# Two attention layers in one planned program: whole-bank writes in the planner for the score maxima, identity products on TensorE before one projection, and a new table of offsets

## The chip, the core and the metric

The kernel runs on one core of one Trainium2 chip. The metric is device time in microseconds (us) of one execution. Several engines work side by side on their own in-order instruction streams: TensorE (PE in the profile, PEld for its weight loads), VectorE (DVE), ScalarE (ACT), GpSimd (POOL) and SyncE (SP), which issues the transfers. PSUM, in which TensorE leaves its results, is used as eight banks of 128x512 float32.

## The reference

Two layers of 2048 tokens, width 1024 and 32 heads of width 32 are computed on separate inputs; their outputs are put side by side.

```python
# A: softmax attention within each of 4 segments of 512 tokens, mixed by a gate with a memory of
#    the segments before
logits = einsum("bhqd,bhkd->bhqk", qs, ks) * scale + mask
a_dot = einsum("bhqk,bhkd->bhqd", softmax(logits), vs)
pq = phi(qs)                                 # phi(t) = t + 1 where t > 0, else exp(t)
a_mem = einsum("bhld,bhde->bhle", pq, M) / (einsum("bhld,bhd->bhl", pq, z)[..., None] + 1e-6)
o = g * a_mem + (1.0 - g) * a_dot
M = M + einsum("bhld,bhle->bhde", phi(ks), vs);  z = z + einsum("bhld->bhd", phi(ks))
...
# B: linear attention with learned features, over all tokens at once
phi_q, phi_k = [concat(softmax(t @ w_phi), softmax(-t @ w_phi)) for t in (q, k)]
kv = einsum("bhsf,bhsd->bhfd", phi_k, v);  z = einsum("bhsf->bhf", phi_k)
o = einsum("bhqf,bhfd->bhqd", phi_q, kv) / (einsum("bhqf,bhf->bhq", phi_q, z)[..., None] + 1e-6)
# each layer ends with o @ wo
```

## The kernel before

**Precision and sizes.** A float32 operand of a large product is held as two float16 halves, and a product of two such operands is three float16 products that add up in one PSUM bank (`product`, the call to TensorE is line 496). Most large products are 128x128 by 128x512. In layer B and in A's output projection, two-by-two block products are made with seven multiplications in place of eight (`strassen`, line 710, and the last loop, line 1805): three banks X, Y and Z are filled, read out by ScalarE and VectorE (lines 716 and 720), and X and Z are then added to again.

**Stages.** Layer A comes first, in 32 units (a segment by a group of four heads), as two functions. `produce(u)` projects queries, keys and values. `attend(u)` finds for each block of queries the largest masked score (`maxima`: products on line 999, VectorE's masked maximum on line 1005, two to four blocks to a bank), turns the 16 maxima of each query into rows that are appended to the operands (line 1024), makes the scores again with the maximum subtracted (line 1104), the exponentials (ACT lines 1108 and 1110, DVE line 1111), the products with the values (line 1140, summed by DVE on line 1144), the normalisation (line 1160), and a transposition by an identity product (line 1172). Preparation of layer B's weights and inputs (`fold`, `prepare`, `weights_v`) is strewn between the units.

Layer B's keys and values follow in eight token pairs: `strassen`, the two softmaxes (`expo`, lines 1395 to 1408), and products that add up the sums over tokens (line 1556; VectorE adds them to `kva`, `ez` and `za` on line 1565).

Then comes the turn from sums to outputs. Each of 16 blocks of 128 queries, numbered c, needs the finished sums: `za` is spread over partitions by float32 identity products (line 1579) into `zb`; the sums `kva` and `ez` (heads 0 to 15 and 16 to 31) are scaled (line 1597) and halved into `kls` (ACT 1599, DVE 1601); the query features `e` of each half hb of the heads are multiplied with `zb` (1710), summed (1713), divided (1716 to 1722), scaled (1724), halved into `eh`, which lies in slot S13 (ACT 1731, and DVE or POOL 1734), transposed by a transfer into `pt` (1737), and multiplied with `kls` (line 1746, 48 short products into the banks `pv` and `kv`: the numerators). Their halves go to `ot` (ACT 1755, DVE 1757), and `project` multiplies `ot` with the output weights: 48 products of line 496 into `misc` banks. While the first of these chains runs, TensorE has the query products of blocks 0 to 3 to make (`strassen`, called for every second c). The output projection of layer A closes the program.

**What sets the order.** The program isn't written in the order in which it runs. Every instruction is recorded by `op` with its engine, an assumed duration, a priority, and what it reads (`r`) and writes (`w`), and `Graph.run` plans them like a list scheduler: an instruction may be placed when, by the assumed durations and latencies, all that it depends on is ready, and the smallest priority goes first. The recorded reads and writes are the planner's alone. The semaphores that the engines wait for are set by the layer below, from the tiles that the instruction really touches. A read or write may name a part of a buffer, as in `(mt, (h, i))`; parts with different keys don't depend on one another. The priority of a job (a run of recorded instructions of one written priority) is shifted by the table `MOVES`, one column of offsets for each engine:

```python
prio += MOVES.get(eng, {}).get(self.job[1], 0.0)
```

The program opens with 56 float32 products of the identity with itself (line 1328), planned at 0.25 us each, while the first inputs are on their way.

Of the kernel before, what the change touches and what calls it, by code (L numbers as in the profile page):

```python
# [379 lines left out]
SP, PE, ACT, DVE, POOL = "SP", "PE", "ACT", "DVE", "POOL"  # L380
# [3 lines left out]
def tile_kernel(ctx: ExitStack, tc: tile.TileContext, ax, aw, awv, awo, beta, bx, bwqk, bwv, bphi, bwo, out):  # L384
    nc = tc.nc
# [71 lines left out]
    op = G.op  # L457
# [512 lines left out]
    def attend(u):  # L970
# [20 lines left out]
        def maxima(*blocks):  # L991
# [11 lines left out]
            for h, i, o in at:  # L1003
                n = 128 * i + 128
                dve(0.073 + 0.001125 * n, lambda h=h, i=i, o=o, n=n: nc.vector.tensor_tensor_reduce(  # L1005
                    ps()[:, o:o + n], ps()[:, o:o + n], causal[:, 512 - n:512], 1.0, NEG, OP.add, OP.max,
                    mt()[:, h, i:i + 1]), w=[(mt, (h, i)), (ps, i)])
# [869 lines left out]
```

## Time and profile before

| | |
|---|---|
| median of 3 runs | 1676.51 us (1674.89 to 1676.59) |
| profiled execution, its own time | 1675.73 us |
| span from first to last instruction in the profile | 1674.0 us |
| mean granted TensorE clock | 0.997 |
| PE busy | 1633.2 us, 98% of the span |
| DVE busy | 1355.2 us, 81% |
| ACT busy | 1120.9 us, 67% |
| POOL busy | 1062.9 us, 63% |

The profile gives each instruction's line, engine, duration, the time its engine was idle before it, and what ended that idle time. A float32 product stands in the trace as two matmul records, so the 56 products of line 1328 are 112 records. The granted clock is TensorE's alone. Times in a window or a timeline are counted from the start of the span. A line of the changed kernel lies 3 lower in the text up to `project` (999 becomes 1002), 6 lower from there to the numerators (1746 becomes 1752), and 10 lower after them.

### The profile page before, as it was taken

How to read it: one execution, taken by the hardware profiler on the slowest of the kernel's cores; microseconds unless marked ns; L12 is line 12 of the kernel's file. 1: busy time of each engine (PE TensorE's matmuls, PEld its weight loads, DVE VectorE, ACT ScalarE, POOL GpSimd, SP SyncE). 2: the span in 40 equal slices, each digit the busy share in tenths (PEclk: the TensorE clock that was granted, in tenths of full speed). 3: DMA queues.
4: the chain of work that ended last, by engine and by line, in shares of the span. 5: the costliest groups of instructions: out<-in, count | busy, mean ns of one | idle time of the engine just before them, and what ended most of it. 6: DMA issues, size and time to landing. Idle time of an engine off the chain costs nothing.

```text
span 1674.0 us, 40119 instructions
## 1 busy us (share of the span) xinstructions
PE 1633.2 (98%) x14964; PEld 963.1 (58%) x14964; DVE 1355.2 (81%) x3187; ACT 1120.9 (67%) x2096; POOL 1062.9 (63%) x1453
## 2 busy tenths in 40 slices
PE   8999999999999999999999999999979999999999
PEld 6666756766676676667665444445534444444444
DVE  6999899998998877798874898778999888964451
ACT  7789979795978878678744676766445555543341
POOL 4667878866689988778541767636478897730000
PEclk9999999999999999999999999999989999999999
DMA  6866765787866576755457364467546768872321
GB/s 211 224 175 151 250 185 169 226 212 191 229 166 210 154 197 210 200 172 157 104 159 274 123 223 164 154 219 283 195 101 166 182 171 183 212 181 99 108 88 69
DMA packets 291410, 299.18 MB, mean 179 GB/s; under 512 B 169088, under 2 KB 222336, under 8 KB 284560
## 3 DMA queue, kind: packets, MB, share of 16 engines
q1 hardware_dynamic: 291216, 296.63, 61.1%
q8 instruction: 117, 1.92, 0.5%
q14 instruction: 77, 0.63, 0.1%
HBM read 161.17 MB, written 86.05 MB: 148 GB/s over the span
## 4 chain that ended last, share of the span: by engine, by line
PE 43%; DVE 5%; ACT 1%; DMA 1%; POOL 0%; issue 0%; DVEq 0%; ACTq 0%
PE proj L710 17%; PE misc L496 9%; PE proj L1805 5%; PE s L710 3%; PE s L1805 2%; PE misc L710 2%; PE misc L1805 1%; PE kv L1556 1%; DVE mx L1395 1%; PE pv L1746 1%; DMA pt<-S 1%; DVE S L1734 1%; DVE pt L1549 1%; DMA wf_d<-oT 0%; DVE r L1405 0%; DVE s L1005 0%
## 5 line engine op out<-in xcount | busy, mean ns | idle before, releaser
L496 PE MATMUL proj<-S,S 128*128 128x128 f16 (+1 forms) x3072 | 500.5, 299 | 2.8 <-ACT S L529 1.2
L496 PEld LDWEIGHTS <-S 128*128 128x128 f16 x4608 | 327.7, 97 | 152.7 <-issue 9.8
L710 PE MATMUL proj<-S,S 128*128 128x512 f16 x1584 | 365.2, 380 | 3.9 <-ACT cs L716 2.4
L710 PEld LDWEIGHTS <-S 128*128 128x128 f16 x2016 | 192.5, 98 | 224.1 <-issue 7.8
L1111 DVE SCALAR_TENSOR_TENSOR ph<-s,ph 128x512 f16<-128x512 f32 x320 | 210.4, 682 | 50.6 <-ACT ph L1110 48.3
L1005 DVE CUSTOM_DVE_ANT_0 s<-s,causal 128x512 f32<-128x512 f32 (+3 forms) x512 | 240.9, 513 | 8.8 <-PE s L999 5.0
L1117 POOL TENSOR_SCALAR_AFFINE_SELECT ph<-ph 128x256 f16<-128x256 f16 (+1 forms) x448 | 195.1, 458 | 76.6 <-DVE ph L1111 58.5
L1110 ACT ACTIVATE ph<-s 128x512 f16<-128x512 f32 x320 | 191.9, 657 | 1.3 <-POOL fo L609 0.4
L496 PE MATMUL misc<-S,ot 128*128 128x512 f16 x768 | 172.2, 379 | 0.0
L1402 ACT ACTIVATE e<-e,sk 128x256 f32<-128x256 f32 x256 | 112.4, 496 | 67.0 <-DVE e L1399 64.2
L496 PEld LDWEIGHTS <-ot 128*128 128x128 f16 x768 | 73.5, 98 | 87.2
L1104 PE MATMUL s<-S 104*128 104x512 f16 (+3 forms) x512 | 117.0, 299 | 2.7 <-DVE amem L1049 0.7
L999 PE MATMUL s<-S 96*128 96x512 f16 (+3 forms) x512 | 111.2, 299 | 3.4 <-ACT pk L952 1.0
L1108 ACT ACTIVATE s<-s,os 128x512 f32<-128x512 f32 x160 | 105.7, 705 | 12.8 <-PE s L1104 12.7
L1108 ACT ACTIVATE s<-s,bd 128x512 f32<-128x512 f32 x160 | 108.0, 721 | 2.5 <-PE s L1104 2.4
L496 PE MATMUL proj<-wv,S 128*128 128x128 f16 x1536 | 108.2, 219 | 0.4 <-DVE ph L1111 0.4
L1140 PEld LDWEIGHTS <-ph 128*128 128x128 f16 x2560 | 87.8, 96 | 20.5 <-issue 2.8
L1140 PE MATMUL pv<-vl,ph 128*128 128x66 f16 (+1 forms) x2560 | 92.3, 184 | 1.5 <-ACT pk L952 0.7
L1405 DVE TENSOR_REDUCE r<-e 128x32 f32<-128x1024 f32 x64 | 76.7, 1207 | 18.0 <-ACT e L1402 17.9
L1710 POOL TENSOR_TENSOR e<-e,zb 128x512 f32<-128x512 f32 x62 | 82.5, 1350 | 12.4 <-ACT zb L1582 7.2
L1005 DVE DVE_READ_ACCUMULATOR2_ANT mt<- 128x1 f32 x512 | 72.4, 141 | 0.0
L1514 POOL TENSOR_TENSOR e<-e,r 128x1024 f32<-128x1024 f32 x32 | 62.1, 1943 | 14.4 <-DVE r L1408 10.0
(345 smaller groups left out, 3259.9 us busy)
## 6 DMA issues: line engine op xcount, KB each, us to landing
S<-xf_d SPq DMA_DIRECT2D x126, 256.0 KB
S<-h SPq DMA_DIRECT2D x192, 128.0 KB
S<-wf_d SPq DMA_DIRECT2D x21, 1024.0 KB
st<-bwqk SPq DMA_DIRECT2D x64, 256.0 KB
out<-os SPq DMA_DIRECT2D x40, 256.0 KB
S<-aw SPq DMA_DIRECT2D x16, 512.0 KB
wa_d<-S SPq DMA_DIRECT2D x16, 512.0 KB
wf_d<-fo SPq DMA_DIRECT2D x32, 256.0 KB
```

Of the source, the lines that this page charges most:

```text
L496: op(PE, dur, lambda c=c, a=a, b=b, lv=lv, rv=rv: nc.tensor.matmul(pv(), lv(), rv(), start=(c == 0 and a + b == 0), stop=(c == n - 1 and a ...
L710: op(PE, 0.215, lambda n=n, a=a, b=b, lv=lv, rv=rv: nc.tensor.matmul(ps(), lv(), rv(), start=(start and n == 0 and a + b == 0), stop=(n == ...
L999: nc.tensor.matmul(ps()[:, o:o + 128 * i + 128], st()[0:96, 0, h, 128 * i:128 * i + 128], st()[0:96, 1, h, 0:128 * i + 128], start=True, s ...
L1005: dve(0.073 + 0.001125 * n, lambda h=h, i=i, o=o, n=n: nc.vector.tensor_tensor_reduce(ps()[:, o:o + n], ps()[:, o:o + n], causal[:, 512 - ...
L1104: nc.tensor.matmul(ps()[:, o:o + n], st()[0:104, 1, h, 128 * j:128 * j + 128], st()[0:104, 0, h, 128 * j:512], start=True, stop=True)
L1108: act(0.59, lambda: nc.scalar.activation(ps(), ps(), AF.Exp, bias=0.0, scale=bdv()[:, 3, i2, 0:1]), r=[(bd, i2)], w=[ps])
L1110: act(0.48, lambda: nc.scalar.activation(ph()[:, 0], ps(), AF.Copy, scale=2.0 ** 14), r=[ps], w=[(ph, 0)])
L1111: dve(0.6, lambda: nc.vector.scalar_tensor_tensor(ph()[:, 1], ps(), 2.0 ** 14, ph()[:, 0], op0=OP.mult, op1=OP.subtract), r=[ps, (ph, 0)], ...
L1117: nc.gpsimd.affine_select(pd, pd, pattern=[[0, n], [1, 128]], compare_op=OP.is_ge, fill=0.0, base=0, channel_multiplier=-1)
L1140: nc.tensor.matmul(ps()[:, i, n0:n1], ph()[:, a, o:o + 128], vl()[:, j, h, n0:n1], start=(i == 0 and a == 0), stop=(j == min(i, 2)), skip_ ...
L1402: op(ACT, 0.41, lambda i=i: nc.scalar.activation(e()[:, 4 * i:4 * i + 4], e()[:, 4 * i:4 * i + 4], AF.Exp, bias=0.0, scale=sk()[:, i:i + 1 ...
L1805: op(PE, 0.215, lambda n=n, a=a, b=b: nc.tensor.matmul(ps(), v(a)[:, n, :], wform[w]()[:, b, n, :], start=(start and n == 0 and a + b == 0 ...
```

## The change

Four edits.

1. In `maxima`, the masked maximum is recorded as a writer of the whole bank and no longer of a part of it. The instruction is the same; in the planner two maxima of one bank now follow one another with the assumed latency of 0.13 us between dependent VectorE instructions.
2. In block c = 0, ahead of each half's numerators, 14 float32 products of the identity with itself are recorded that write the numerators' bank `pv`, which the numerators then overwrite. For the planner they read both lower parts of that half's `eh`.
3. In block c = 0, ahead of the projection's first product, 10 more of the same kind write its `misc` bank. For the planner they read the lower parts of the second half's `eh`.
4. The whole table `MOVES` has other numbers. The set of other instructions stays: the counts by line are equal on every engine but TensorE, which has 38 more.

The products of edits 2 and 3 are planned at 0.11 us each. The matmul itself touches only `ident` and the bank, so that no wait for `eh` is built from it.

```diff
 MOVES = {
     "DVE": {
-        0: -8.8, 4: -25.3, 7: 1.6, 8: -0.7, 10: -2.9, 12: -20.2, 13: 24.6, 14: -1.3, 15: -10.6, 16: -16.6, 17: 0.6, 18: 0.7,
...
+        0: -9.7, 4: -16.8, 7: -26.6, 9: 18.9, 10: 0.1, 12: -0.5, 13: 19.3, 14: 7, 15: -2.1, 16: 6.5, 17: -4.1, 18: 41.3,
...
@@ maxima
                     ps()[:, o:o + n], ps()[:, o:o + n], causal[:, 512 - n:512], 1.0, NEG, OP.add, OP.max,
-                    mt()[:, h, i:i + 1]), w=[(mt, (h, i)), (ps, i)])
+                    mt()[:, h, i:i + 1]), w=[(mt, (h, i)), ps])
@@ project
-    def project(o, w, row, col, prio):
+    def project(o, w, row, col, prio, warm=None):
         for n in range(2):
             ps = bank("misc", [128, 512])
+            for _ in range(0 if warm is None or n else 10):
+                op(PE, 0.11, lambda ps=ps: nc.tensor.matmul(ps()[:, 0:128], ident, ident, start=True, stop=True),
+                   r=warm, w=[ps], prio=prio)
             product((ps, ps), o, at(w[n]), NG, prio, dur=0.215)
@@ the numerators, for each half hb of block c
+            if c == 0:
+                for _ in range(14):
+                    op(PE, 0.11, lambda pn=pn, hb=hb: nc.tensor.matmul(pn[0]()[:, 2 * hb, :], ident, ident, start=True, stop=True),
+                       r=[(eh, (hb, 1, 0)), (eh, (hb, 1, 1))], w=[pn[0]], prio=P)
             op(PE, 0.5, f, r=[(kls, (0, hb)), (kls, (1, hb)), pt], w=pn, prio=P)
@@ the projection of block c
-        project(lambda a, g: (ot, None, lambda otv=otv: otv()[:, a, g, :]), bo, c * 128, 1024, P + 1.1)
+        project(lambda a, g: (ot, None, lambda otv=otv: otv()[:, a, g, :]), bo, c * 128, 1024, P + 1.1, None if c else [(eh, (1, 1, 0)), (eh, (1, 1, 1))])
```

The order moves everywhere. Three places matter here. The first is TensorE's stream just ahead of the first numerators of block 0, in the kernel before; `proj` is a bank of the query products, `pv` and `kv` are the numerators' banks:

```order
L710 MATMUL proj<-S_19191,S_15152 128x512
L710 LDWEIGHTS S_15152
L710 MATMUL proj<-S_19191,S_15152 128x512
L1746 LDWEIGHTS kls
L1746 MATMUL pv<-pt,kls 32x128
```

and in the changed one:

```order
L713 LDWEIGHTS S_15102
L713 MATMUL proj<-S_19242,S_15102 128x512
L1758 MATMUL pv<-ident 128x128 x14
L1621 MATMUL misc<-ident 128x128 x10
L713 LDWEIGHTS S_15102
L713 MATMUL proj<-S_19242,S_15102 128x512
L713 LDWEIGHTS S_15102
L713 MATMUL proj<-S_19242,S_15102 128x512
L713 LDWEIGHTS S_19695
L713 MATMUL proj<-S_19357,S_19695 128x512
L1752 LDWEIGHTS kls
L1752 MATMUL pv<-pt,kls 32x128
```

The ten products that were recorded for the projection stand here too, ahead of the first numerators, since the second half's `eh` was planned to be ready early. Ahead of these rows there are 103 query products after the last key sums, and 104 before. The other 14 stand between the two halves' numerators.

The second place is TensorE's stream right behind the second half's numerators, before:

```order
L1746 LDWEIGHTS kls
L1746 MATMUL kv<-pt,kls 32x128
L710 LDWEIGHTS S_14196
L710 MATMUL proj<-S_19002,S_14196 128x512
```

and now:

```order
L1752 LDWEIGHTS kls
L1752 MATMUL kv<-pt,kls 32x128
L499 LDWEIGHTS ot
L499 MATMUL misc<-S_19831,ot 128x512
```

Before, 12 query products, the numerators of block 1 and 12 more query products stood between block 0's numerators and its projection; now the projection (48 products, `misc` from `ot`) follows at once, and the numerators of block 1 come behind it.

The third place is VectorE's stream from the last but few instructions to the second part of `kls` (`ez` is the second half's sum, `mx`, `e` and `r` are of the query softmax, `S13` is `eh`), before:

```order
L1601 TENSOR_TENSOR kls_19785<-kva_16712,kls_19785 128x512
L1395 TENSOR_REDUCE mx_20009<-proj_19636 128x16 x2
L1399 TENSOR_TENSOR e_20066<-mx_20009,proj_19636 128x16x32
L1734 TENSOR_TENSOR S13_19903<-e_19759,S13_19903 128x512
L1597 TENSOR_TENSOR ez_16875<-ez_16875,zr_19773 128x512
L1405 TENSOR_REDUCE r_20074<-e_19988 128x32
L1734 TENSOR_TENSOR S13_19903<-e_19574,S13_19903 128x512
L1601 TENSOR_TENSOR kls_19785<-ez_16875,kls_19785 128x512
```

and now:

```order
L1604 TENSOR_TENSOR kls_19787<-kva_16748,kls_19787 128x512
L1740 TENSOR_TENSOR S13_19952<-e_19499,S13_19952 128x512 x2
L1600 TENSOR_TENSOR ez_16903<-ez_16903,zr_19755 128x512
L1400 TENSOR_TENSOR e_19989<-s_19897,mx_19943 128x16x32
L1402 TENSOR_TENSOR e_19989<-mx_19943,s_19897 128x16x32
L1398 TENSOR_REDUCE mx_20007<-proj_19675 128x16
L1402 TENSOR_TENSOR e_20019<-mx_20007,proj_19675 128x16x32
L1604 TENSOR_TENSOR kls_19787<-ez_16903,kls_19787 128x512
```

From the last write of `za` to this second part of `kls`, VectorE had 56 instructions before and has 50 now; two of block 1's lower halves (`S13` from `e_19759` and `e_19574` before) have moved behind it, and so have four reductions of line 1395 and one bank addition of line 720. The start of the program (the 56 products and the first products after them) is unchanged on TensorE.

225 rows, old and new, of the table MOVES are left out of this document.

## The prediction

> **What bounds the kernel now.** I read the busy shares first, then TensorE's busy time by stage, then its waits, and last the one stage that stands out, instruction by instruction. The page's first part:
>
> ```profile
> PE 1633.2 (98%) x14964; PEld 963.1 (58%) x14964; DVE 1355.2 (81%) x3187; ACT 1120.9 (67%) x2096; POOL 1062.9 (63%) x1453
> ```
>
> TensorE is the bound: all its idle time together is 1674.0 - 1633.2 = 40.8 us, 2.4% of the span. No reordering can gain much more, and products that are added anywhere but in idle time cost their whole length. By stage (window, PE busy, PEld, DVE, ACT, POOL, granted clock, DMA):
>
> ```profile
> 0.00:850.00 850.00, 826.66 (x8890) 573.42 (x8891) 744.26 (x2146) 686.54 (x1260) 639.93 (x1011) 1.00 0.67 189
> 850.00:1200.00 350.00, 348.65 (x2526) 179.73 (x2525) 275.29 (x500) 219.80 (x446) 193.45 (x205) 1.00 0.60 201
> 1200.00:1250.00 50.00, 38.36 (x348) 17.13 (x347) 47.53 (x81) 22.70 (x47) 36.15 (x38) 0.90 0.49 138
> 1250.00:1650.00 400.00, 399.64 (x3116) 184.08 (x3114) 285.91 (x459) 188.41 (x340) 193.40 (x201) 1.00 0.56 150
> 1650.00:1674.00 24.00, 19.91 (x93) 8.78 (x90) 2.25 (x3) 3.44 (x5) 0.00 (x0) 1.00 0.17 66
> ```
>
> TensorE idles 23.3 us in layer A's first 850 us, 1.4 in the key stage, 11.6 in the 50 us of the turn, 0.4 in the outputs and 4.1 at the end. Only the first and the third can give anything. In the first the idle time is crumbs; the largest groups of the waits (total, times, longest):
>
> ```profile
> PE misc L1024 <- POOL mh L1022: 3.6, 8, 1.2
> PE pv L1746 <- ACT kls L1599: 3.4, 1, 3.4
> PE pv L1746 <- DVE kls L1601: 2.8, 2, 2.2
> PE misc L1328 <- DVE ident L416: 2.6, 1, 2.6
> PE proj L710 <- ACT cs L716: 2.4, 3, 1.4
> PE pv L1746 <- DMA pt<-S: 2.0, 2, 1.8
> PE proj L710 <- DVE s L720: 1.5, 1, 1.5
> ...
> PE s L999 <- DVE ph L1111: 0.9, 1, 0.9
> ```
>
> In the turn it is a few long waits, and a slow clock. TensorE's timeline (start, length, work, idle before it):
>
> ```profile
> 1200.31 9.66 PE L710 MATMUL proj<-S,S 128*128 128x512 f16 x44
> 1211.47 7.93 PE L710 MATMUL proj<-S,S 128*128 128x512 f16 x36 [1.50 <-DVE s L720]
> 1220.83 2.75 PE L710 MATMUL proj<-S,S 128*128 128x512 f16 x12 [1.43 <-ACT cs L716]
> 1224.33 2.75 PE L710 MATMUL proj<-S,S 128*128 128x512 f16 x12 [0.74 <-ACT cs L716]
> 1228.87 0.23 PE L1746 MATMUL pv<-pt,kls 64*32 64x128 f16 x1 [1.79 <-DMA pt<-S]
> ...
> 1229.74 0.23 PE L1746 MATMUL pv<-pt,kls 64*32 64x128 f16 x1 [0.57 <-DVE kls L1601]
> ...
> 1233.56 0.29 PE L1746 MATMUL pv<-pt,kls 64*32 64x128 f16 x1 [3.39 <-ACT kls L1599]
> ...
> 1236.18 0.28 PE L1746 MATMUL pv<-pt,kls 64*32 64x128 f16 x1 [2.21 <-DVE kls L1601]
> ...
> 1236.74 4.67 PE L710 MATMUL proj<-S,S 128*128 128x512 f16 x12
> ```
>
> Beside it VectorE's last write of the key sums and its last part of `kls`, and the issues of the transposing transfers:
>
> ```profile
> 1199.00 0.15 DVE L1565 SCALAR_TENSOR_TENSOR za<-kv,za 128x4 f32<-128x4 f32 x1
> ...
> 1234.49 1.63 DVE L1601 TENSOR_TENSOR kls<-ez,kls 128x512 f16<-128x512 f32 x1
> ```
>
> ```profile
> 1224.40 4.44 SPq L1737 DMA_TRANSPOSE pt<-S  x2
> ```
>
> The seven waits are 1.50 + 1.43 + 0.74 + 1.79 + 0.57 + 3.39 + 2.21 = 11.6 us, the whole idle time of that stage. Behind them 12 products take 4.67 us where 12 took 2.75. The windows say why:
>
> ```profile
> 1227.00:1230.40 3.40, 0.80 (x49) 0.38 (x48) 3.40 (x5) 2.40 (x6) 2.07 (x2) 1.00 1.14 211
> 1230.40:1240.60 10.20, 4.83 (x58) 1.91 (x59) 10.13 (x15) 5.96 (x14) 7.60 (x6) 0.50 0.74 161
> 1240.60:1244.00 3.40, 3.40 (x62) 1.66 (x61) 2.52 (x4) 0.59 (x2) 2.29 (x5) 1.00 0.27 77
> ```
>
> Behind 3.4 us in which TensorE was busy for 0.80, the clock is halved for 10.2 us; 4.83 us of work stood in them and would have taken 2.4. So the turn loses 11.6 + 2.4 = 14.0 us.
>
> **The change part by part.**
>
> *The identity products.* One product costs what the opening's do:
>
> ```profile
> 13.65 4.71 PE L1328 MATMUL misc<-ident 128*128 128x128 f32 x40
> ```
>
> That is 20 products in 4.71 us, their 40 records less than 0.12 apart: 0.23 us each, about twice the 0.11 us that the planner was told. The 24 ahead of the first numerators take 5.5 us, the 14 between the halves 3.2, together 8.7. They wait for no other engine: their reads of `eh` are the planner's, so they run when TensorE arrives. Before, it arrived at 1224.33 + 2.75 = 1227.1. Of the waits ahead of that, 1.43 and 0.74 were for a bank's read-out between two multiplications into one bank; the new order puts 8 other products (8 x 0.22 = 1.8 us, the rate of the 44 in 9.66) into each of those places, so both waits go. The 1.50 stays, as I see nothing that moves it. Arrival is then about 1224.7 (a query product less), the 24 end at 1230.2, three query products follow, and the first numerators start at 1230.9.
>
> Are they ready then? VectorE ran without a pause there (47.53 of 50 us), so I step through its rows. Lower parts of the first half: the steps of the rows from `za` to there sum to 21.8 us before (0.6 for 512 elements, 1.13 for 1024, 0.1 to 0.26 for the short ones) and took about 25.2, since some rows lasted longer while POOL ran (below). Now the steps sum to 22.9, so some 26.3, at 1225.4; the transfers took 1228.87 - 1224.40 = 4.5 us to land, so `pt` is there at 1229.9. Ready. Second part of `kls`: the steps summed to 31.0 and took 37.0 (1236.12 - 1199.15); now they sum to 26.5, so about 32, at 1231.2 to 1232.2. The row of 1.63 us at 1234.49 shows the stretching: its work is 0.6, the rest lies under this POOL row:
>
> ```profile
> 1234.15 1.42 POOL L1734 TENSOR_TENSOR S<-e,S 128x512 f16<-128x512 f32 x1 [2.46 <-ACT S L1731]
> ```
>
> The first numerators take 0.5, the 14 products 3.2, so the second numerators start at 1234.6, ready, and end at 1235.1, against 1236.8 before. Here the 3.39 and 2.21 are gone, and so is the reason for the half clock.
>
> What is late next is the projection, which now follows at once. `ot` needs two ACT and two DVE rows behind the numerators:
>
> ```profile
> 1236.87 0.60 ACT L1755 ACTIVATE ot<-pv 128x512 f16<-128x512 f32 x1 [2.85 <-PE kv L1746]
> ...
> 1238.11 0.68 DVE L1757 SCALAR_TENSOR_TENSOR ot<-kv,ot 128x512 f16<-128x512 f32 x1
> ```
>
> 1238.79 less the 1236.8 at which the numerators ended, and 0.2 to TensorE: 2.2 us of idle time. Before, 12 query products covered it; now nothing does, since the ten products meant for it stand ahead of the first numerators. Behind it 48 products run, long enough for block 1's numerators.
>
> The turn then loses 8.7 (added products) + 1.5 + 2.2 = 12.4 in place of 14.0: **-1.6 us**. Bounds: if VectorE's rows come early enough that neither the 1.5 nor the 2.2 is left, -5.3; if `kls` comes as late as before (1236.1), TensorE idles 1.5 more, and if the clock is halved as well, 10.2 us of dense work lose up to 5.1: +5.0.
>
> *The whole-bank rule and the offsets in layer A.* The rule changes no instruction. In the new order a bank's two maxima mostly have one of another bank between them. VectorE's rows there cost:
>
> ```profile
> L1005 DVE CUSTOM_DVE_ANT_0 s<-s,causal 128x512 f32<-128x512 f32 x128 | 91.8, 717 | 5.0 <-PE s L999 5.0
> ```
>
> Its time is the same in either order; only the bank is held for one row longer. The offsets can take away at most the stage's idle time less the opening's 2.62 and 1.2, some 19.5 us, and can add as much again. I compared, in TensorE's stream, the work that stands between products that hang together through other engines: the least between a unit's rows and its scores is 6.9 us of products now and was 6.2, between scores and their value products 4.3 against 3.0; between the last maxima product and the rows 3.0 against 3.3, where the waits of line 1024 arise. Two of three have more room, none much. VectorE, at 744 of 850 us the second bound, has 13 to 20 us less work ahead of the ends of units 15 and 17, and 7 more ahead of those of units 1 and 18 (the order's instructions, each at its line's busy time over its count). I take a tenth of the crumbs: **-2 us**, with -8 and +8 as ends. Key stage, outputs and end have 1.4, 0.4 and 4.1 us of idle time and the same loops: 0.
>
> *Sum.* -1.6 - 2.0 = -3.6 on the profiled execution's 1675.73, which gives 1672.1; that execution was 0.8 below the median of the runs, so **1673** against the median of 1676.5.
>
> *A rule against this.* The Trainium skill (TensorE: Matmul & The Clock Gate, section "HAM oscillation — how this bites in real kernels") has it that only an idle gap over about 3.4 us brings the half clock. By that the wait of 1.79 us needed no cover: the 24 products ahead of the first numerators are 5.5 us for nothing but the waits that they happen to fill, and the 14 alone would do. The trace disagrees on the threshold: the clock fell at 1230.4, a few tenths into the 3.39 us wait, behind a stretch that was a quarter busy. By the rule the new 2.2 us gap is harmless; by the row it is not certainly so.
>
> **The rivals.**
>
> *The clock falls all the same*, in the projection's wait: 2.2 us idle and half a microsecond of numerators could make a 3.4 us stretch as thin as the 0.80 above. Then up to 5.1 us come back: 1678. Against it: the identity products are dense up to the numerators, so such a stretch is some 35% busy.
>
> *Slower: a bank held too long.* The whole-bank rule makes the short maximum stand behind another bank's longest, 0.72 us later. Where TensorE has no spare `s` bank, its next maxima or scores wait. This can happen 4 times in each of 32 units; it decides from about one in ten: 13 x 0.72 = 9 us, 1682. For it: TensorE already waits on VectorE at line 999 (0.9 us above), and the work between a unit's first and last maxima product grew from 6.7 to 7.7 us in the middle. Against it: the planner holds banks by the same rule, so that it sees the wait.
>
> *The order pays off in layer A.* With VectorE's early load lightened, half of the 19.5 us go: 1666.
>
> *The change does nothing that can be told.* The waits move and the identity products cost what the clock gave: 1676.5.
>
> **How the numbers follow.** Forecast, a small gain at 1673: 0.47 (0.27 faster, 0.20 the same). Clock falls, 1678: 0.13 (0.09 the same, 0.04 slower). Bank held, 1682: 0.17, slower. Layer A pays off, 1666: 0.15, faster. Nothing, 1676.5: 0.08 (0.01, 0.05, 0.02). With 0.2% (3.4 us) as what can be told from no change: faster 0.43, the same 0.34, slower 0.23. The forecast's own range is 1669 to 1677; the unknown ends and the rivals on both sides make it 1664 to 1683.
>
> **What would show it.** Right: identity products of 0.23 us, the clock at 1.00 throughout the turn, no wait of over 2.5 us at the numerators, a wait of about 2 us for `ot` at the projection, and some 21 us of idle time in the first 850. Wrong: a granted clock of 0.5 in the turn; numerators that still wait for `kls`; idle time at lines 999 and 1104 that grows on VectorE's account; or a first half that moves by more than 8 us, which would mean that the table, of which I can judge least, decides.

## The result, and the profile after

| | before | after |
|---|---|---|
| median of the runs beside each other | 1676.55 us (1674.89 to 1678.01, 6 runs) | 1665.64 us (1664.21 to 1666.33, 6 runs) |
| span of the profiled execution | 1674.0 us | 1663.4 us |
| ratio of the times, 95% interval | | 0.9937 [0.9927, 0.9947] |

The change makes the kernel faster by 10.9 us. A small gain to 1673 was forecast: the direction is right, and the gain is three times as large as forecast. The result lies outside the forecast's own range of 1669 to 1677, and inside the whole range of 1664 to 1683 that the rivals made, near its lower end.

The page's first part for the changed kernel:

```profile
PE 1636.6 (98%) x15040; PEld 971.7 (58%) x15040; DVE 1345.6 (81%) x3187; ACT 1119.8 (67%) x2096; POOL 1062.7 (64%) x1453
```

TensorE's idle time fell from 40.8 us to 1663.4 - 1636.6 = 26.8, while its busy time rose by 3.4 with the identity products. The stages, in the windows of the kernel before (columns: window, PE busy, PEld, DVE, ACT, POOL, granted clock, DMA share, GB/s):

```profile
0.00:850.00 850.00, 831.56 (x9036) 580.46 (x9037) 745.78 (x2174) 694.56 (x1274) 642.37 (x1023) 1.00 0.68 191
850.00:1200.00 350.00, 349.84 (x2427) 177.66 (x2426) 268.75 (x493) 217.77 (x442) 194.03 (x197) 1.00 0.60 203
1200.00:1250.00 50.00, 46.51 (x427) 25.82 (x425) 43.33 (x69) 20.19 (x41) 38.91 (x42) 0.97 0.42 107
```

Idle in them: 18.4, 0.2 and 3.5 us, against 23.3, 1.4 and 11.6. Read like that, the turn would seem to have given the most, 8.1 us. It has not: TensorE is busy there with products that are not part of the result. What a stage gave is read from a mark at its end. The last product of the key sums (line 1556) ends 10.2 us earlier than before (1187.2 against 1197.4), and the last product of the program 10.6 us earlier (1659.4 against 1669.9). Nearly all the gain is made **before the turn begins**.

To see where, I took for each TensorE instruction the time from its start to the start of the next, less the median of that step for the same line and shape in the kernel before, and summed it by stage. This counts a stretched step as lost, which a sum of idle time does not. Layer A loses 35.6 us where it lost 44.7 (units 0 to 7: 20.1 against 19.7; 8 to 15: 6.5 against 10.4; 16 to 23: 5.2 against 8.8; 24 to 31: 3.8 against 5.8), the key stage 1.3 against 2.5. So 9.1 us come from layer A and 1.2 from the key stage. In layer A the loss at line 1024 went from 6.9 to 4.8, at 1140 from 4.1 to 2.6, at 1067 from 2.8 to 1.0, at 1042 from 2.9 to 1.4, at 1104 from 6.4 to 5.3, and at 999 from 7.6 up to 9.1. No single place gave more than 2.1 us. In a second execution of the changed kernel (below) layer A loses 37.2 us by the same sum, 7.5 less than before.

The waits of the changed kernel (total, times, longest) hold nothing on `kls` any more, where the longest waits of before were:

```profile
PE misc L1027 <- POOL mh L1025: 2.8, 6, 0.9
PE proj L713 <- DVE s L723: 2.7, 1, 2.7
PE misc L1331 <- DVE ident L419: 2.6, 1, 2.6
PE s L1002 <- ACT pk L955: 1.5, 2, 0.9
...
PE misc L499 <- ACT ot L1765: 0.7, 1, 0.7
```

The turn in TensorE's timeline (start, length, work, idle before it), with the identity products on lines 1758 and 1621:

```profile
1189.44 14.46 PE L713 MATMUL proj<-S,S 128*128 128x512 f16 x65
1206.58 9.70 PE L713 MATMUL proj<-S,S 128*128 128x512 f16 x38 [2.68 <-DVE s L723]
1216.12 3.29 PE L1758 MATMUL pv<-ident 128*128 128x128 f32 x28
1219.25 2.40 PE L1621 MATMUL misc<-ident 128*128 128x128 f32 x20
1221.48 0.81 PE L713 MATMUL proj<-S,S 128*128 128x512 f16 x3
1222.75 3.39 PE L1758 MATMUL pv<-ident 128*128 128x128 f32 x28
1227.37 10.83 PE L499 MATMUL misc<-S,ot 128*128 128x512 f16 x48 [0.70 <-ACT ot L1765]
```

The numerators (line 1752) run in the two places ahead of the second 3.39 us and ahead of the projection, without a wait of over 0.2 us. One wait has grown: the 2.68 us at line 713 were 1.50 before. Behind it the granted clock is half (0.50 in the second window):

```profile
1202.50:1205.90 3.40, 1.41 (x7) 0.54 (x6) 3.40 (x8) 0.57 (x2) 1.52 (x3) 1.00 0.21 62
1205.90:1209.30 3.40, 2.72 (x7) 1.01 (x7) 3.40 (x10) 1.62 (x4) 3.09 (x8) 0.50 0.83 328
1209.30:1216.00 6.70, 6.70 (x33) 3.03 (x31) 6.70 (x7) 2.78 (x5) 6.54 (x5) 1.00 0.15 40
```

### The profile page after: what moved, and what is told of

It reads as the page before. It is cut to its first block, busy times and chain, and to the rows that moved or that the text cites. A ratio compares the mean times of both kernels' runs of the same rounds, so it can differ in the third digit from the quotient of the medians.

```text
span 1663.4 us, 40321 instructions
## 1 busy us (share of the span) xinstructions
PE 1636.6 (98%) x15040; PEld 971.7 (58%) x15040; DVE 1345.6 (81%) x3187; ACT 1119.8 (67%) x2096; POOL 1062.7 (64%) x1453
## 4 chain that ended last, share of the span: by engine, by line
PE 59%; DVE 12%; ACT 7%; POOL 4%; issue 3%; DMA 2%; SPq 0%; ACTq 0%; DVEq 0%; POOLq 0%
PE proj L713 16%; PE proj L499 11%; PE misc L499 7%; PE proj L1815 5%; PE s L713 3%; PE s L1815 2%; PE pv L1143 2%; PE s L1107 2%; DVE s L1008 2%; ACT ph L1113 2%; PE s L1002 2%; PE misc L713 2%; ACT s L1111 2%; DVE ph L1114 1%; PE misc L1815 1%
## 5 line engine op out<-in xcount | busy, mean ns | idle before, releaser
L499 PE MATMUL proj<-S,S 128*128 128x512 f16 (+1 forms) x3072 | 499.1, 299 | 3.3 <-ACT S L532 1.2
L1120 POOL TENSOR_SCALAR_AFFINE_SELECT ph<-ph 128x256 f16<-128x256 f16 (+1 forms) x448 | 198.7, 466 | 93.3 <-DVE ph L1114 81.7
L1008 DVE CUSTOM_DVE_ANT_0 s<-s,causal 128x512 f32<-128x512 f32 (+3 forms) x512 | 236.1, 522 | 7.3 <-PE s L1002 7.3
L1113 ACT ACTIVATE ph<-s 128x512 f16<-128x512 f32 x320 | 186.6, 629 | 1.1
L1111 ACT ACTIVATE s<-s,bd 128x512 f32<-128x512 f32 x160 | 103.6, 678 | 11.3 <-PE s L1107 8.5
L499 PE MATMUL proj<-wv,S 128*128 128x128 f16 x1536 | 104.7, 219 | 0.1
```

Of the source, the lines that this page charges most:

```text
L499: op(PE, dur, lambda c=c, a=a, b=b, lv=lv, rv=rv: nc.tensor.matmul(pv(), lv(), rv(), start=(c == 0 and a + b == 0), stop=(c == n - 1 and a ...
L1111: act(0.59, lambda: nc.scalar.activation(ps(), ps(), AF.Exp, bias=0.0, scale=bdv()[:, 3, i2, 0:1]), r=[(bd, i2)], w=[ps])
L1113: act(0.48, lambda: nc.scalar.activation(ph()[:, 0], ps(), AF.Copy, scale=2.0 ** 14), r=[ps], w=[(ph, 0)])
L1120: nc.gpsimd.affine_select(pd, pd, pattern=[[0, n], [1, 128]], compare_op=OP.is_ge, fill=0.0, base=0, channel_multiplier=-1)
```

## The experiments

Four questions were open. Do the identity products pay? Which part of the change made the gain in layer A? Is it the rule or the table? And is VectorE's lateness what the new order cured? All times stand against runs of the kernel before on the same chip (medians 1675.6 to 1676.0 in the three sets of experiments). The place of a gain is read from the two marks above, relative to the profiled execution of before:

| kernel | median, us | ratio, 95% interval | last key sum | last product |
|---|---|---|---|---|
| the change | 1665.64 | 0.9937 [0.9927, 0.9947] | -10.2 | -10.6 |
| the change, once more | 1665.76 | 0.9934 [0.9922, 0.9947] | -8.6 | -9.9 |
| ... without identity products | 1668.35 | 0.9957 [0.9943, 0.9970] | -10.5 | -10.4 |
| ... without, beside the repeat | 1667.00 | 0.9945 [0.9932, 0.9957] | -8.2 | -6.7 |
| before, 14 identity products | 1674.97 | 0.9993 [0.9984, 1.0002] | +0.9 | -0.8 |
| before, new rule and layer A's offsets | 1667.43 | 0.9955 [0.9942, 0.9968] | -10.6 | -9.3 |
| ... with 14 identity products | 1666.13 | 0.9941 [0.9928, 0.9955] | -10.1 | -12.5 |
| before, the rest of the change | 1693.05 | 1.0102 [1.0087, 1.0116] | 0.0 | +14.9 |
| before, new rule alone | 1761.52 | 1.0512 [1.0492, 1.0532] | +76.9 | +86.3 |
| no offsets, old rule | 1717.40 | 1.0244 [1.0228, 1.0261] | +30.3 | +37.9 |
| no offsets, new rule | 1700.86 | 1.0148 [1.0133, 1.0162] | +16.3 | +23.5 |
| before, shorter VectorE rows | 1674.60 | 0.9990 [0.9981, 0.9998] | -3.4 | -2.4 |
| the change, shorter VectorE rows | 1667.73 | 0.9949 [0.9937, 0.9961] | -6.9 | -6.3 |

A mark of one order moves between two executions (-10.2 and -8.6 in the first two rows, -10.5 and -8.2 in the next two; the last product of those two even -10.4 and -6.7), so differences of marks of 2 us or so say nothing.

### Layer A apart from the rest

The kernel before with the whole-bank rule and with the new offsets of layer A's jobs only; the offsets from the key stage on are the old ones, and there are no identity products:

```diff
-                    mt()[:, h, i:i + 1]), w=[(mt, (h, i)), (ps, i)])
+                    mt()[:, h, i:i + 1]), w=[(mt, (h, i)), ps])
 MOVES = {
     "DVE": {
-        0: -8.8, 4: -25.3, 7: 1.6, 8: -0.7, 10: -2.9, 12: -20.2, 13: 24.6, 14: -1.3, 15: -10.6, 16: -16.6, 17: 0.6, 18: 0.7,
+        0: -9.7, 4: -16.8, 7: -26.6, 9: 18.9, 10: 0.1, 12: -0.5, 13: 19.3, 14: 7, 15: -2.1, 16: 6.5, 17: -4.1, 18: 41.3,
...
```

> The kernel before with the whole-bank rule and the new offsets for layer A's jobs alone (up to job 234 of 399); the jobs of layer B and of the outputs keep the old offsets, and there are no identity products. Theory (layer A's order brings some 9 us, as the time that TensorE loses between its products fell from 44.7 to 35.6 us by the end of unit 31): 1667, between 1664 and 1671. Rival (the gain needs the new turn or the identity products): 1674 to 1677.

It takes 1667.43 us, and its key sums end 10.6 us early, as early as in the whole change. In its trace the order of TensorE, VectorE, ScalarE and GpSimd is that of the changed kernel, instruction by instruction, up to 917 us, behind the end of layer A, and that of the kernel before from 1057 us on. So its turn is still that of before, with the same waits for `pt` and `kls` and a half clock in them:

```profile
1218.50:1221.90 3.40, 0.55 (x48) 0.24 (x32) 3.37 (x6) 2.44 (x5) 1.23 (x2) 1.00 1.02 251
1221.90:1228.80 6.90, 3.58 (x55) 1.47 (x56) 6.90 (x11) 3.62 (x8) 5.19 (x4) 0.51 0.83 154
```

So the rule and layer A's part of the table bring some 8 to 9 of the 10.9 us, with the turn and the outputs in the old order.

The complement was tried as well: the old rule and the old offsets up to the middle of the key stage, the new offsets behind, and the identity products. (The ten jobs 235 to 244, of the key stage, have the old offsets in both runs.)

```diff
 MOVES = {
     "DVE": {
         0: -8.8, 4: -25.3, 7: 1.6, 8: -0.7, 10: -2.9, 12: -20.2, 13: 24.6, 14: -1.3, 15: -10.6, 16: -16.6, 17: 0.6, 18: 0.7,
...
-        245: 3.6, 249: 3.5, 250: 8.2, 252: -34.5, 254: -16.9, 255: -0.3, 257: 21.3, 261: 4.1, 262: -4.6, 264: 33.2,
+        245: -75.5, 249: -3.8, 250: 2, 252: 54.3, 254: 77.6, 255: 2.4, 257: 51, 259: -20.2, 261: 2.5, 262: 14.2,
...
```

> The complement: the kernel before with its own offsets and its own rule for the maxima up to job 244, the new offsets behind that, and the identity products. Theory: the new turn and key stage are worth 1 to 2 us together: 1675, between 1672 and 1677. Rival (the turn and the identity products bring the gain): 1666 to 1669.

The expectation missed: 1693.05 us, 17 slower than before. Layer A and the key stage are as before (0.0 at the last key sum); the loss arises in the turn and the outputs. With the same offsets there, its second part comes out in another order than in the changed kernel; why the new offsets do not carry over was not followed up. So this run is no measure of what the second part of the change is worth; the difference between the whole change and the run above is the better one, 1.8 us.

### The identity products

The changed kernel without them, in the same order (they do not enter the result):

```diff
-            lambda ps=ps: nc.tensor.matmul(ps()[:, 0:128], ident, ident, start=True, stop=True)
+            lambda: None
...
-            lambda pn=pn, hb=hb: nc.tensor.matmul(pn[0]()[:, 2 * hb, :], ident, ident, start=True, stop=True)
+            lambda: None
```

> The changed kernel without its 38 identity products; every other instruction of every engine stands in the same order. In the changed kernel's trace TensorE comes to them at 1216.1 us, makes 24 (5.7 us) and 3 query products, and the first numerators run at 1222.2; the transposed features are issued at 1216.96, and by the 4.5 us that this took before they land at 1221.4. Theory (the gain lies in layer A's order, the identity products pay for themselves about): without them TensorE idles some 4.6 us here, the projection begins up to 2.9 us earlier, and the clock is halved for 3.4 to 10.2 us, which costs 1.7 to 5.1: 1664.5 to 1668, against 1665.6 with them. Rival (the identity products bring most of the 10.9 us): 1673 to 1676.

Its timeline (numerators, then projection) and its windows:

```profile
1221.09 0.28 PE L1752 MATMUL pv<-pt,kls 64*32 64x128 f16 x1 [5.86 <-DMA pt<-S]
...
1224.99 12.51 PE L499 MATMUL misc<-S,ot 128*128 128x512 f16 x48 [0.71 <-ACT ot L1765]
```

```profile
1215.20:1218.60 3.40, 0.03 (x1) 0.00 (x0) 3.40 (x4) 0.36 (x1) 2.30 (x3) 1.00 0.24 45
1218.60:1228.90 10.30, 5.59 (x105) 2.40 (x106) 10.08 (x16) 5.77 (x12) 6.20 (x6) 0.50 0.58 115
```

TensorE now waits 5.86 us for `pt`, the clock is halved for 10.2 us, and the projection takes 12.51 us in place of 10.83. On the other side the projection starts 2.4 us earlier, since no products delay the numerators. It ends at 1237.5 here and at 1238.2 with the products: in these two traces they are worth nothing up to there. The medians (1668.35 and 1665.64) came from different sets of runs, so both kernels were run once more beside each other:

> The changed kernel once more, beside the same without its identity products. Theory (the identity products are worth nothing: what they cost is what the clock and the waits gave): 1666, within 2 us of the other. Rival (they are worth the 2.7 us by which the two medians of different chips differed): 1665.6 here, the other at 1668.4.

> The changed kernel without its 38 identity products, in the same order. Theory: 1666 to 1667, no difference from the changed kernel beside it that the intervals tell. Rival (the half clock of 10.2 us costs more than 8.6 us of products): 1668.4, 2.7 above it.

1665.76 against 1667.00. The difference of 1.2 us lies within the intervals of the two ratios, [0.9922, 0.9947] and [0.9932, 0.9957]. The trace of the repeat without the products shows the half clock behind the wait for `pt` again, for three steps of 3.4 us:

```profile
1218.50:1221.90 3.40, 0.54 (x3) 0.05 (x1) 3.40 (x5) 0.76 (x2) 1.43 (x1) 1.00 0.59 111
1221.90:1232.10 10.20, 6.52 (x108) 2.71 (x109) 9.99 (x16) 5.37 (x11) 7.13 (x6) 0.50 0.56 113
```

Next the products without the rest of the change: 14 in the kernel before, between the two halves' numerators of block 0, where it waited 3.39 us for `kls`.

```diff
             def f(pn=pn, pt=pt, hb=hb, c=c):
+                for _ in range(14 if c == 0 and hb == 1 else 0):
+                    nc.tensor.matmul(pn[0]()[:, 2 * hb, :], ident, ident, start=True, stop=True)
                 for n in range(2):
```

> The kernel before with one thing added: 14 identity products between the two halves' numerators of block 0, with no other instruction moved. There TensorE waited 3.39 and 2.21 us, and the clock was halved from 1230.4 to 1240.6, which cost 2.4 us. Theory (the clock follows TensorE's share of busy time in stretches of 3.4 us, and the numerators wait for the halves of the key sums in any case): the products hide in the wait of 5.6 us, the clock is half for one stretch of 3.4 us at most, and the kernel gains the 2.4 us: about 1674. Rival (they only cost, 14 x 0.23 us): 1677 to 1680. Rival (nothing, since the clock falls as before): 1676.5.

The ratio, 0.9993 [0.9984, 1.0002], does not tell it from no change, but the trace shows what was expected of the clock. The half clock lasts 3.4 us in place of 10.2, and falls on the identity products alone; the 12 query products behind them take 2.76 us, where they took 4.67:

```profile
1231.02 5.02 PE L1742 MATMUL pv<-ident 128*128 128x128 f32 x28
...
1237.45 2.76 PE L710 MATMUL proj<-S,S 128*128 128x512 f16 x12
```

Last, the same 14 products in the kernel with only layer A's part of the change:

> The kernel before with the new rule and the new offsets of layer A alone, and 14 identity products between the halves' numerators of block 0 in their longest wait. Theory (the two gains lie in different stages and add up: -9 in layer A, -1 to -2 in the turn): 1665.5, no worse than the changed kernel beside it; the half clock lasts 3.4 us in place of 6.8. Rival (products in that wait push the projection back by what the clock gives): 1667.4, as without them.

1666.13 us; no half clock is left in its turn (one row for the 60 us around it), where the kernel without the 14 had 6.9 us of it:

```profile
1200.00:1260.00 60.00, 51.65 (x520) 25.31 (x520) 57.87 (x99) 29.04 (x58) 47.47 (x51) 1.00 0.50 111
```

That is the time of the whole change (1665.76 beside it) with 14 identity products in place of 38, and with the old offsets from the key stage on. Over the four comparisons of with and without (2.7, 1.2, 1.0 and 1.3 us) the products always came out ahead, none of them by more than the intervals allow for chance, and the first and the last between different sets of runs: a gain of some 1 to 2 us is likely and not settled.

### The rule or the table

The whole-bank rule alone, with the old offsets:

```diff
-                    mt()[:, h, i:i + 1]), w=[(mt, (h, i)), (ps, i)])
+                    mt()[:, h, i:i + 1]), w=[(mt, (h, i)), ps])
```

> The kernel before with the whole-bank rule alone, its own offsets kept, no identity products. Theory (the gain is an order of rule and offsets fitted to one another, found as a whole): the old offsets no longer fit the banks, the first 850 us lose something, 1680 or more. Rival 1 (the rule is what gave the 9 us in layer A): 1667. Rival 2 (the rule by itself moves little): 1676.5.

1761.52 us, 86 slower. Its waits begin with

```profile
PE pv L1746 <- DMA pt<-S: 23.5, 6, 16.7
PE misc L1172 <- POOL osum L1167: 7.8, 2, 7.4
PE s L999 <- DVE mt L1005: 7.0, 17, 0.8
PE misc L1024 <- DVE dm L1048: 6.1, 1, 6.1
```

and its windows in layer A show the clock at half in part of them:

```profile
0.00:318.00 318.00, 300.69 (x3065) 208.24 (x3066) 268.32 (x811) 258.33 (x468) 221.68 (x362) 0.98 0.65 180
318.00:560.00 242.00, 210.47 (x2193) 145.25 (x2191) 195.94 (x511) 160.15 (x300) 139.61 (x237) 0.92 0.66 182
560.00:795.00 235.00, 224.27 (x2298) 150.32 (x2296) 172.65 (x522) 175.45 (x321) 184.79 (x272) 0.96 0.60 169
```

The third of these waits is the rival of the prediction, TensorE at line 999 behind a maximum that holds its bank: 17 times and 7.0 us, where the kernel before has it once for 0.2 and the changed kernel once for 0.4. But it is a small part of 86 us. To separate the rule's own price from the misfit with the old offsets, both rules were run without any offsets:

```diff
-MOVES = {
-    "DVE": {
...
+MOVES = {}
```

> The kernel before with no offsets at all, the planner's own due times, old rule. Theory (the offsets, fitted to the rule, carry the order): far slower than before, by 50 us or more, 1730 to 1800. Rival (the planner's due times are nearly as good): within 15 us, 1690.

> No offsets, with the whole-bank rule. Theory (the 86 us of the rule beside the old offsets are the misfit of the two, not the price of holding a bank longer): within 15 us of the kernel without offsets and without the rule. Rival (holding the banks longer is what costs): 50 us or more slower than that one.

The table is worth 42 us to the kernel before (1717.40 against 1675.81), somewhat less than the 50 or more expected. Without a table the rule is no burden but a gain, 1700.86 against 1717.40: not the equal time that was expected, and the other way round than the rival. The wait that the rival named is shorter with the rule; in the waits of the two (here line 881 is line 999 of before, and 887 is 1005), without the rule and then with it:

```profile
PE s L881 <- DVE mt L887: 7.4, 6, 3.8
```

```profile
PE s L881 <- DVE mt L887: 1.9, 3, 1.3
```

So the rule can lengthen that wait or shorten it, by what stands around it. What the change brings belongs to the rule and the offsets together: 86 us are lost where the one is taken without the other. (The new table beside the old rule was not measured: the planner finds no order for it.)

### VectorE's lateness

The prediction's rival for layer A said that the new order pays off by lightening VectorE's early load. If the crumbs there are TensorE waiting for late VectorE rows, shorter rows should do the same. In both kernels, in their own order, the lower parts of the attention weights are left out:

```diff
-            nc.vector.scalar_tensor_tensor(ph()[:, 1], ps(), 2.0 ** 14, ph()[:, 0], op0=OP.mult, op1=OP.subtract)
+            nc.vector.tensor_scalar(ph()[:, 1], ph()[:, 0], 0.0, None, op0=OP.mult)
```

> The kernel before, its order as it is, with VectorE's lower parts of the attention weights left out: each of the 512 rows that subtract the upper part from the exponentials (0.68 us) becomes a product of the upper part and zero, so the lower parts are zero in the result; some 0.4 us of VectorE less per row, 150 to 200 us in all. Theory (the crumbs of layer A are TensorE waiting for VectorE's late rows, and the new order pays off since its rows come earlier): most of the 25 us that TensorE loses in units 8 to 31 go, 1658. Rival (the crumbs come from other engines and from the order of TensorE's own products): at most 4 us less, 1672 to 1676.

> The changed kernel with the same rows of VectorE shortened, the lower parts zero in the result. Theory (VectorE's lateness is what the new order lessened): little is left to gain, 1657, within 3 us of the kernel before so shortened. Rival: the difference of 10 us between the two kernels stays, 1662 to 1666.

There are 320 such rows, not the 512 of the expectation, and they shortened by less than expected, so VectorE lost 50 us of work and not 150 to 200 (the group of these rows, at the line that took 682 ns before, and the page's first line, both of the kernel before so shortened):

```profile
L1111 DVE TENSOR_SCALAR ph<-ph 128x512 f16<-128x512 f16 x320 | 155.3, 499 | 73.2 <-ACT ph L1110 70.3 <-POOL ph L1117 1.4
```

```profile
PE 1632.3 (98%) x14964; PEld 962.1 (58%) x14964; DVE 1305.0 (78%) x3187; ACT 1118.5 (67%) x2096; POOL 1071.4 (64%) x1453
```

Those 50 us bring the kernel before 1.2 us (0.9990 [0.9981, 0.9998]) and bring the changed kernel nothing (1667.73, against 1665.76 in another set; expected were 1657, or by the rival 1662 to 1666). In units 8 to 31, where the new order gained, the loss of the kernel before goes from 25.0 to 23.5 us; the new order took it to 15.6. (In units 0 to 7, where the new order gained nothing, it goes from 19.7 to 17.4.) The theory falls as far as it was tried: the length of these rows does not set the crumbs that the new order removed, although the shortened row no longer reads the scores' bank and so does not hold it either. The rows now wait longer for ACT (70.3 us ahead of this line, 48.3 before), so part of the time saved went into waiting for ScalarE. Other rows of VectorE were not shortened.

## Why the prediction was right, and where it was wrong

**The direction was right, the sum was not.** The sum put 1.6 us in the turn and 2 in layer A; the runs show 8 to 9 in layer A and 1 to 2 behind it. That 1665.64 still lies in the whole range is owed to the room left there for the rival of layer A, and in so far it is luck.

**The step that failed is "I take a tenth of the crumbs: -2 us".** Layer A gave 9.1 us by the start-to-start sum in one execution and 7.5 in another (with the key stage, at the last key sum, 10.2 and 8.6). This lies about at the bound of -8 that was set. There were two errors in it. The pool was drawn too small: it counted 19.5 us of idle time, while TensorE loses another half in steps that are stretched without a gap that the profile calls idle (of the 44.7 us, 21.0 are gaps and 23.7 are longer steps; of the 35.6 after, 15.8 and 19.8). And the share of the gaps was a quarter, 5.2 of 21.0, and not a tenth: it was set by looking for one mechanism in the order, and there is none that is large. The gain is 1 to 2 us at each of five lines. The prediction's own test for this, "a first half that moves by more than 8 us, which would mean that the table, of which I can judge least, decides", came true in the first execution, and nearly in the second.

**The rival "the order pays off in layer A" had the size right**, 1666 us, with a chance of 0.15. The reason it gave got no support: VectorE's rows, made 50 us shorter by hand, brought the old order 1.2 us. What delays TensorE at each of these places in the old order stays open. That rule and offsets must be taken together, and that layer A holds the gain, is shown; which engine's offsets do it is not.

**The turn: its terms were wrong, its total is not settled.** Forecast were 12.4 us of loss in place of 14.0, a gain of 1.6. In the changed kernel's trace there are 9.1 us of identity products (3.29 + 2.40 + 3.39; forecast 8.7), the wait at line 713 with 2.7 (forecast to stay at 1.5), 1.4 for the half clock behind it (2.72 us of work at half speed, forecast none), and 0.7 at the projection (forecast 2.2): 13.8 us, a gain of 0.2. In the repeat the half clock is missing and 0.46 us of waiting for `pt` is added: 12.9, a gain of 1.1. From the last key sum to the last product the change gained 0.4 us in the first trace and 1.3 in the repeat, which is less than marks move between executions; the medians of layer A's part alone and of the whole differ by 1.8, within their intervals.

- *The projection's wait*: I took it that the first of the 48 products needs both halves of `ot`. It starts behind ACT's row, and VectorE's half is read later; the wait is 0.70 us.
- *"The 1.50 stays, as I see nothing that moves it"*: it became 2.68, and 2.67 in the repeat. TensorE came to the identity products 28.9 us behind the last key sum and not 27.3, as forecast; the longer wait (1.2) and the half clock (1.4) more than account for it. Why the wait grew was not followed up.
- *The numerators*: forecast to be ready when TensorE arrives, and they were: no wait for `kls`. The lower parts of `eh` came 28.8 us behind `za`, not 26.3, and `pt` landed at 1221.6, 0.6 us before the numerators that read it. In the repeat `pt` was late by 0.46 us. The second part of `kls` was ready 33.5 us behind `za`, in the forecast 32 to 33. The rows:

```profile
1188.02 0.15 DVE L1568 SCALAR_TENSOR_TENSOR za<-kv,za 128x4 f32<-128x4 f32 x1
...
1216.96 4.64 SPq L1743 DMA_TRANSPOSE pt<-S  x2
...
1221.01 0.68 DVE L1604 TENSOR_TENSOR kls<-ez,kls 128x512 f16<-128x512 f32 x1
```

- *The clock at 1.00 throughout the turn*: true from the identity products on, and wrong ahead of them in one of two executions. In the repeat the same wait, 2.67 us, left the clock alone. What tells the cases apart is where the wait falls on the clock's own steps. In each trace the clock changes only at whole multiples of 3.41 us from its other changes. Counted so, the step with the wait held 1.40 us of TensorE's work in the changed kernel, and the half clock came behind it; in the repeat it held 1.41, and the clock stayed; in the first run without the identity products the same wait (2.66 us) was cut in two by the end of a step, with 2.01 and 2.15 us of work, and the clock stayed too. The changed kernel, its repeat, and the run without the products:

```profile
1202.51:1205.92 3.41, 1.40 (x7) 0.53 (x6) 3.41 (x8) 0.59 (x2) 1.53 (x3) 1.00 0.22 65
...
1206.10:1209.51 3.41, 1.41 (x7) 0.68 (x7) 3.41 (x10) 2.19 (x5) 3.06 (x5) 1.00 0.89 312
1209.51:1212.92 3.41, 3.41 (x18) 1.54 (x16) 3.41 (x7) 0.75 (x2) 3.31 (x5) 1.00 0.19 77
...
1201.55:1204.96 3.41, 2.01 (x10) 0.79 (x9) 3.41 (x7) 0.00 (x0) 1.53 (x3) 1.00 0.11 16
1204.96:1208.37 3.41, 2.15 (x10) 0.97 (x10) 3.41 (x8) 2.19 (x5) 3.10 (x8) 1.00 0.94 366
```

The Trainium skill (TensorE: Matmul & The Clock Gate, section "HAM oscillation — how this bites in real kernels") gives as its rule that TensorE should have no idle gap over about 3.4 us. The traces show the half clock behind less: behind the 2.68 us in the changed kernel, and in the kernel before 0.2 us into the wait of 3.39 us, behind a step whose longest finished wait is 1.79 us. The prediction's weighing of it ("not certainly so") was apt for such a gap, but it looked at the projection's gap and not at this one.

**The rival "the clock falls anyway"** did not happen in the projection's wait. The clock fell in another place, in one of two executions, for 3.4 us rather than 10.2, and cost 1.4 us and not 5.1.

**The rival "a bank held too long"** is a mechanism that exists: 17 waits and 7.0 us where the rule meets the old offsets, close to its 13 x 0.72 = 9. Beside the new offsets it does not arise: line 999 loses 1.5 us more, and its waits on a maximum are 0.4 us. The argument against it, that the planner sees the wait, is what held.

**Idle time in the first 850 us** was forecast at some 21 and is 18.4.

## What to carry to other kernels

Where an order comes from a planner and a table of fitted offsets, a rule of the planner and the table are one edit: taken alone, a rule that is worth 16.5 us without offsets cost 86 with the old ones. When asked what a new order can give, measure TensorE's loss from start to start and not by idle time, since half of it here was in stretched steps; and when no mechanism is found, widen the bound rather than take a tenth. Products that only keep the clock up paid here about what they cost: 38 of them came out 1.2 and 2.7 us ahead, 14 in the longest wait 1.0 and 1.3, none of it clear of chance.

## What was not expected of the hardware

- In one trace all changes of TensorE's clock lie whole multiples of 3.413 us apart (in the changed kernel at 7.84, 1205.92, 1209.33 and 1663.30 us, which is 351, 1 and 133 steps), and the half clock lasts 3.41, 6.83 or 10.24 us in the turns, and 23.89 us in that of the new rule alone. These steps begin at another point of the span in each execution. So the same wait of 2.7 us brings the half clock in one execution and not in the next. In the 70 us behind the last key sum, in all 14 traces, the 12 steps at full clock with at most 1.40 us of TensorE's work were followed by the half clock, and none with 1.41 us or more was. Elsewhere the bound is another: in layer A, with the new rule alone, the half clock also came behind steps with up to 2.20 us of work.
- VectorE's f16 rows that read and write f16 alone take very different times: 228 ns at the least, 338 in the median, 1401 at the most, in the view of that line:

```profile
L1111 DVE TENSOR_SCALAR ph<-ph x320: 228/338/1401, 77.3 to 889.4; 128x512 f16<-128x512 f16 x160
```

Of the 320, the 43 that no POOL row overlaps take 258 to 296 ns, and the 183 that POOL rows cover to nine tenths or more take 446 in the median. The rows that they replaced, which read PSUM, take 626 to 693 with or without POOL beside them. So these short rows were long where POOL rows lay beside them; no run here takes the POOL rows away. With the 320 rows in place of 512, this is why the experiment took off a quarter to a third of what was expected.
